# A delta-rule attention kernel with routed experts: the router's logits stay where the product leaves them, one row write a chunk, and a newly sought order

## The chip, the core and the metric

The kernel runs on one core of a Trainium2 chip. The metric is device time of one execution in microseconds (us); lower is better.

## What is computed

First, for 4 batches and 8 heads, a delta-rule attention over 768 steps with head size 48: with the key k normalised, y_t = q_t S, then S = S + beta_t k_t (v_t - S k_t). The heads' outputs, joined, are x with 384 columns per token. Then a mixture of 8 experts. logits = x w_gate; a local gate (one more column of weights) says whether a token takes the arg max of its own logits or the expert of the token before it in its sequence, so the choice is a running "last fresh choice" along the sequence. The output row is p[e] * relu(x w1[e]) w2[e], with p the softmax of the token's logits at its expert.

## The kernel before, in words

**Attention.** The 768 steps are 12 chunks of 64 steps; two chunks form a pair (0 to 5). A chunk's tokens lie on the 128 partitions as 64c+32a+t (c: which batch of two, a: which half of the chunk, t: step in the half), with a free index j for the other batch bit. For each pair a unit-triangular system is solved step by step (lines 293 to 306, "S" operations, 31 steps of two operations, 15 for pair 0). A table `MODE` says on which engine: all pairs on POOL (GpSimd), pair 3 on DVE (VectorE). Behind the solve stand transposes (lines 311, 314) and small products that make `XT` (lines 339 to 367). The chunks are then run in sequence by `online` (line 373): products with the state (fk, fq), the difference R (line 383), the product with `XT` (p1, line 391), the copy Us (line 397), the new state (p3, lines 400 to 404), the output (p2, lines 406 to 411) into the tile `y`. All these matmuls are issued through line 213.

**A chunk's way to the router.** `y` is written to the row table `xs` in DRAM by four transfers (line 415), transposed by one transfer into `xt` (line 417), multiplied with the router's weights (`lf`, line 422), and two DVE operations (line 438) put the logits into the tile `lt`, of which there is one. Eight transfers (line 442) then carry `lt` into `lg`, whose layout has one 32-step piece of one batch on 32 partitions. The last chunk writes `lg` without transfers: its product (`lf2`, line 429) is cut into 48 small matmuls, each aimed at its own 32 partitions. All these transfers are issued by SP (SyncE) in one queue.

**Routing** (lines 617 to 748) runs in two halves: the first when 8 chunks (16 columns of `lg`) are there, the second at the end. A half takes arg max and gates (629 to 637), finds the last fresh choice along the sequence by a transpose, a scan, a product with a block matrix (645) and a second scan (648), gives each token its expert and rank, and makes index lists for the gathers. Line 719 multiplies the exponentials with the chosen expert's mask; the planner may put it on DVE or POOL. 256 tokens of the first expert run behind the first half, the rest behind the second; from expert 2 on (`rest`) the order is fixed by hand.

**What sets the order.** A list scheduler (`Sched.order`) gives each operation an engine and a place when the program is built; on the chip each engine runs its own list in order and waits where an input is late. It uses estimated durations: 60 ns of SP for a transfer's issue, 2000 ns plus bytes over 330 bytes/ns to landing, and a model of TensorE's instruction fetch and clock. Between operations that could start it picks by the longest path behind them plus the offsets of the table `RANK` (by kind of operation and chunk), with `PACE` as a wished distance between successive p1. Buffers are given out in the same pass.

Of the kernel before, what the change touches and what calls it, by code (L numbers as in the profile page):

```python
# [36 lines left out]
class Op:  # L37
    def __init__(s,fn,bufs,e,c):
        s.lock=0; s.pc=None; s.fn=fn; s.bufs=bufs; s.e=e; s.c=c if isinstance(c,dict) else {x:c for x in e}
        s.pre=set(); s.succ=[]; s.end=None; s.iss=60.; s.takes=fn.__code__.co_argcount>len(fn.__defaults__ or ())  # L40

class Sched:


    HOP=70; DMA=2000; BW=330.; LOOK=120; WIN=3413.; UP=4.3; DN=3.6; FQ=128; FL=96; FT=2800.
# [28 lines left out]
    def span(s,o,t):  # L74

        if not o.pc: return o.c['P']
        c,w,n,q=o.pc; k=int(t//s.WIN)
        while len(s.hot)<=k:
            m=len(s.hot)-1; s.hot.append(s.act.get(m,0)>=(s.DN if s.hot[m] else s.UP))
        d=(w if s.hot[k] else c)/q; a,b=s.got,s.got+q; s.got=b; e=t  # L80
        while a<b:
            z=a%s.FQ; y=min(b,a-z+(s.FL if z<s.FL else s.FQ))
            if z==0: s.got_at=e
            if z==s.FL: e=max(e,s.got_at+s.FT)
            e+=d*(y-a); a=y
        return e-t
# [5 lines left out]
    def order(s):  # L92
        s.hot=[False]; s.act={}; s.got=0; s.got_at=0.
        s.rank(); E={x:0. for x in 'VAGPSL'}; dma=0.; out=[]; left={}; s.when=[]
# [54 lines left out]
class Attn:  # L149
# [3 lines left out]
    NKV=3; NW=14; NAMP=6; NG2=6; NXT=3; NLX=2; NUS=2; PACE=7526.1; MODE=((16,'G'),(32,'G'),(32,'G'),(32,'D'),(32,'G'),(32,'G'))  # L153
    RANK={'':{-1: -330.6},
# [50 lines left out]
    def build(s,extra=(),pre={},post=None):  # L205
# [167 lines left out]
        def online(n):  # L373
# [49 lines left out]
            def lf2():  # L423
                for a in range(2):
                    for b in range(4):
                        j,c=divmod(b,2); o=slice(64*c+32*a,64*c+32*a+32)
                        for z in range(2):
                            for kk in range(3):
                                nc.tensor.matmul(p.t[32*b:32*b+32,18*a:18*a+18-9*z],xt.t[:,6*j+3*z+kk,o],wv(kk,z),start=(z==0 and kk==0),stop=(z==1 and kk==2),skip_group_check=True,tile_position=(0,32*b))
            last=n==N-1  # L430
            add(lf2 if last else lf,r=[xt,"wc"],w=[p],e='P',c=900); S.ops[-1].pc=(900,850,.2,48) if last else (800,700,.6,12); C["lf"]=S.ops[-1]
            pv=lambda:p.t[:,0:36].rearrange("p (b w e) -> p b w e",b=2,w=2); lk=[("lg",2*n),("lg",2*n+1)]
            if last:
                def fg(): v=pv(); o=s.lg[:,2*n:2*n+2,:]; nc.vector.tensor_scalar_mul(o,v[:,:,0,:],2.0**-16); nc.vector.scalar_tensor_tensor(o,v[:,:,1,:],2.0**-16,o,op0=ALU.mult,op1=ALU.add)
                add(fg,r=[p],w=lk,c=370); s.lastfg=S.ops[-1]
            else:
                lt=s.lt()
# [22 lines left out]
class Moe:  # L460
# [14 lines left out]
    def consts(s):  # L475
# [119 lines left out]
    def graph(s,S,A):  # L595
# [21 lines left out]
        for z,(lo,hi) in enumerate(((0,SP),(SP,NS))):  # L617
# [27 lines left out]
            add(lambda pt=pt,dg=dg,n=n:nc.tensor.matmul(pt.t[:,0:n],s.blk,dg[:,0:n],start=True,stop=True),r=["sc"+Z,CK],w=[pt],e='P',c=450)  # L645
# [1 line left out]
            def fc(pt=pt,n=n,lo=lo,hi=hi,sl=sl,scT=scT,z=z):
                V.tensor_tensor_scan(s.cs[:,lo+1:hi+1],s.one.to_broadcast([128,n]),pt.t[:,0:n],0.0 if z==0 else s.cs[:,lo:lo+1],ALU.mult,ALU.max)
                V.tensor_tensor(s.ei[:,sl],scT[:,0:n],s.cs[:,lo:hi],op=ALU.max)
# [1 line left out]
            add(fc,r=[pt,"st"+Z,CK]+(["cs0"] if z else []),w=["cs"+Z,"ei"+Z],c=600)
# [3 lines left out]
            if z==0:  # L655
# [361 lines left out]
```

## Time and profile before

| | |
|---|---|
| median of 3 runs | 549.89 us (541.59, 550.07, 549.89) |
| profiled execution | 541.3 us, span 539.6 us, mean granted TensorE clock 0.819 |
| PE (matmul) / DVE / ACT / POOL busy | 409.8 / 337.6 / 188.5 / 234.6 us |
| transfers `lg<-lt`, `xs<-y`, `xt<-y` | 88, 48, 12 issues |

The span has two parts. Up to about 306 us attention and routing run, with all engines partly idle. From there the experts' matmuls follow each other closely. Times in rows count from the span's start. An engine name with q (SPq) is the engine's sequencer, which issues transfers and waits. In brackets behind a row of a timeline stands how long the engine idled before it and what ended that.

### The profile page before, as it was taken

To read this page: it belongs to the slowest core of one execution; us is meant where nothing else is said; L and a number is where in the kernel's file an instruction comes from. 1 tells how busy PE (TensorE), PEld (TensorE's weight loads), DVE (VectorE), ACT (ScalarE), POOL (GpSimd) and SP (SyncE) were. 2 spreads that over 40 slices of the span, in tenths; PEclk is the share of its full clock that TensorE was granted. 3 is DMA by queue.
4 is the path that set the end of the run, shared out by engine and by line. 5 is a ranking of instruction groups with operands and counts; after the bars stand their busy time and mean duration, and the time that the engine had idled before them with its cause. 6 is when DMAs were issued, how large, how long until landed. Compare 5 with 4: busy or idle time off the path is not lost. (4 is left out here: it accounts for less than half of the span.)

```text
span 539.6 us, 19450 instructions
## 1 busy us (share of the span) xinstructions
PE 409.8 (76%) x8459; PEld 304.6 (56%) x8459; DVE 337.6 (63%) x727; ACT 188.5 (35%) x332; POOL 234.6 (43%) x411
## 2 busy tenths in 40 slices
PE   4635785763766676677788598789999998999992
PEld 4534674752665676576675574354655555555661
DVE  3897145788985733693458545617666886778540
ACT  5323246424347343424540124305234251525210
POOL 5488889820797896141001543123141505040301
PEclk9665588796597665565599699899999999999997
DMA  8920054474275375255532295235655666385300
GB/s 329 388 91 5 5 121 106 122 183 113 82 232 126 94 194 114 55 125 114 168 91 60 76 201 178 81 122 156 176 169 151 197 162 205 101 251 138 73 16 26
DMA packets 68280, 72.78 MB, mean 135 GB/s; under 512 B 46771, under 2 KB 58095, under 8 KB 68192
## 3 DMA queue, kind: packets, MB, share of 16 engines
q1 hardware_dynamic: 64640, 61.45, 41.6%
q0 software_dynamic: 3552, 10.06, 5.9%
q8 instruction: 67, 1.10, 0.8%
q14 instruction: 21, 0.17, 0.1%
HBM read 52.63 MB, written 10.05 MB: 116 GB/s over the span
## 5 line engine op out<-in xcount | busy, mean ns | idle before, releaser
L298 POOL TENSOR_TENSOR fg<-L,X 128x31 f32<-128x31 f32 (+15 forms) x124 | 67.8, 547 | 35.3 <-DVE X L283 25.8
L299 POOL TENSOR_TENSOR X<-X,fg 128x31 f32<-128x31 f32 (+15 forms) x124 | 71.5, 577 | 9.7
L566 PEld LDWEIGHTS <-W 128*128 128x128 f16 (+2 forms) x408 | 41.5, 102 | 25.2 <-issue 0.5
L561 DVE TENSOR_SCALAR gf<-pr 128x384 f32<-128x384 f32 (+6 forms) x72 | 39.9, 556 | 24.5 <-ACT W L560 11.9
L559 PE MATMUL pr<-kv,amp 128*128 128x448 f16 (+4 forms) x192 | 53.9, 357 | 0.7 <-DVE tx L842 0.4
L213 PE MATMUL pr<-W 64*64 64x128 f32 x768 | 33.4, 329 | 22.8 <-DMA W<-in_kq_dram 11.5
L213 PE MATMUL pr<-S,W 64*64 64x48 f32 x1408 | 37.9, 273 | 13.0 <-issue 5.4
L213 PEld LDWEIGHTS pr<-S,W 64*64 64x64 f32 x1408 | 34.4, 188 | 16.2 <-issue 6.7
L213 PEld LDWEIGHTS pr<-W 64*64 64x64 f32 x768 | 29.1, 168 | 25.2 <-issue 8.0
L559 PE MATMUL pr<-kv,W 128*128 128x384 f16 (+2 forms) x144 | 38.0, 345 | 5.1 <-DVE tx L842 2.4
L559 PEld LDWEIGHTS <-W 128*128 128x128 f16 x288 | 29.4, 103 | 17.3 <-issue 4.0
L560 ACT ACTIVATE W<-pr 128x224 f16<-128x224 f32 (+3 forms) x32 | 15.5, 484 | 66.8 <-PE pr L559 64.8
L549 POOL DMA_INDIRECT out_dram<-y,so x9 | 10.7, 1187 | 53.4 <-DVE y L576 53.4
L547 POOL DMA_INDIRECT G<-xs,gi x25 | 26.2, 1050 | 13.0 <-issue 6.7
L213 PE MATMUL pr<-R,xtp 64*64 64x48 f32 x704 | 30.0, 251 | 1.8 <-issue 1.7
L213 PEld LDWEIGHTS pr<-R,xtp 64*64 64x64 f32 x704 | 28.8, 169 | 2.2 <-issue 2.2
L559 PEld LDWEIGHTS <-amp 128*128 128x128 f16 x192 | 18.8, 98 | 18.9 <-issue 1.9
L544 DVE SCALAR_TENSOR_TENSOR W<-W,W 128x768 f16<-128x768 f32 (+1 forms) x19 | 21.0, 1104 | 11.5 <-ACT W L542 11.4
L213 PE MATMUL pr<-Us,amp 64*64 64x48 f32 x768 | 19.2, 259 | 10.0 <-ACT Us L397 9.2
L549 POOL DMA_INDIRECT out_dram<-S,so x8 | 11.2, 1403 | 31.2 <-DVE S L576 29.3
L560 ACT ACTIVATE xtp<-pr 128x384 f16<-128x384 f32 (+2 forms) x16 | 8.4, 526 | 45.7 <-PE pr L559 41.1
L213 PEld LDWEIGHTS pr<-Us,amp 64*64 64x64 f32 x768 | 17.6, 174 | 11.8 <-ACT Us L397 10.8
(359 smaller groups left out, 987.1 us busy)
## 6 DMA issues: line engine op xcount, KB each, us to landing
W<-in_kq_dram SPq DMA_DIRECT2D x24, 512.0 KB, 6.5
W<-in_moe_w_dram SPq DMA_DIRECT2D x22, 512.0 KB, 4.9
W<-in_moe_w_dram SPq DMA_DIRECT2D x28, 384.0 KB, 3.3
kv<-in_kv_dram SPq DMA_DIRECT2D x12, 768.0 KB, 5.1
xs<-y SPq DMA_DIRECT2D x48, 96.0 KB, 2.8
amp<-in_moe_w_dram SPq DMA_DIRECT2D x4, 384.0 KB, 3.6
lg<-lt SPq DMA_DIRECT2D x88, 1.1 KB, 2.5
amp<-in_moe_w_dram SPq DMA_DIRECT2D x2, 512.0 KB
```

Source lines behind the costliest of these rows:

```text
L213: mm=lambda o,l,r,st,sp,tp:MM(o,l,r,start=st,stop=sp,skip_group_check=True,tile_position=tp)
L298: eng.tensor_tensor(tv,l[:,j,j+1:].unsqueeze(2).to_broadcast([128,n,k]),x[:,j,0:k].unsqueeze(1).to_broadcast([128,n,k]),op=ALU.mult)
L299: eng.tensor_tensor(x[:,j+1:,0:k],x[:,j+1:,0:k],tv,op=ALU.subtract)
L544: def wlo(s,st,w,k): s.nc.vector.scalar_tensor_tensor(s.wv(w,k)[:,1],s.wst(st,k),256.0,s.wv(w,k)[:,0],op0=ALU.mult,op1=ALU.subtract)
L547: return s.nc.gpsimd.indirect_dma_start(out=x[0:m],out_offset=None,in_=s.xs[0:nt,:],in_offset=bass.IndirectOffsetOnAxis(ap=ix[0:m],axis=0) ...
L549: I=s.nc.gpsimd.indirect_dma_start(out=s.out[:,:],out_offset=bass.IndirectOffsetOnAxis(ap=ix[0:m],axis=0),in_=y[0:m],in_offset=None,bounds ...
L559: for k in range(3): s.nc.tensor.matmul(ps,s.wv(W[k],k)[:,a,0,128*f:128*f+128],xT[:,3*b+k,:],start=(x==0 and k==0),stop=(x==2 and k==2))
L560: def uphi(s,h,ps): s.nc.scalar.activation(h,ps,AF.Relu,scale=2.0**-6)
L561: def upt(s,t,ps): s.nc.vector.tensor_scalar(t,ps,0.0,2.0**-6,op0=ALU.max,op1=ALU.mult)
L566: s.nc.tensor.matmul(po[0:m],h(a,f)[:,c:c+m],s.wv(W[k],k)[:,b,f%2,:],start=(x==0 and f==0),stop=(x==2 and f==7))
```

## The change

Every chunk's logits are now written by the two DVE operations straight into `lg`, in the layout that the product leaves (partition 64c+32a+t, column 2n+j). `lt`, its 88 transfers and the cut product `lf2` are gone; the last chunk uses the same 12 matmuls as the others. The row table follows the same layout, so a chunk's rows go out with one transfer in place of four. The routing is adapted: the mask `dm` is doubled to tell the two half-pieces apart, the block matrix covers 64 columns, the product of line 645 has twice the columns, and the function `fc` has three DVE operations more (a copy, a masked maximum, and the scan done once for each j). Constants (`first`, `s8`, `vals`, `am`) follow the layout. The planner counts 430 ns for a transfer's issue (1490 for the transpose, before 1700), includes all matmuls in its model of the instruction fetch and lets a fetch wait for transfers; `PACE` and `RANK` have new values, so the place of any operation up to the hand-ordered part can differ. `MODE` is as before.

```diff
 class Op:
-        s.lock=0; s.pc=None; s.fn=fn; ...
+        s.lock=0; s.pc=None; s.q=24; s.fn=fn; ...
-        ... s.iss=60.; ...
+        ... s.iss=430.; ...
 class Sched:
-    ... FT=2800.
+    ... FT=2400.; FD=450.
     def span(s,o,t):
-        if not o.pc: return o.c['P']
-        c,w,n,q=o.pc; k=int(t//s.WIN)
+        c,w,n,q=o.pc or (o.c['P'],o.c['P'],0.,o.q); k=int(t//s.WIN)
...
-            if z==0: s.got_at=e
+            if z==0: s.got_at=max(e+s.FD,s.dma)
...
-    ... PACE=7526.1; MODE=((16,'G'),(32,'G'),(32,'G'),(32,'D'),(32,'G'),(32,'G'))
+    ... PACE=11107.4; MODE=((16,'G'),(32,'G'),(32,'G'),(32,'D'),(32,'G'),(32,'G'))
-    RANK={'':{-1: -330.6},
...
+    RANK={'':{-1: 91.5, 0: -760.0},
...
-            for c in range(2):
-                for a in range(2):
-                    add(lambda c=c,a=a:nc.sync.dma_start(s.xs[2*n+a].rearrange(...)[c],y.t[64*c+32*a:64*c+32*a+32]...),...,c=98304)
+            add(lambda:nc.sync.dma_start(s.xs[2*n:2*n+2].rearrange("j p e -> p j e"),y.t.rearrange("p j z c -> p j (z c)")),...,c=393216)
-            def lf2(): ...
-            last=n==N-1
-            add(lf2 if last else lf,r=[xt,"wc"],w=[p],e='P',c=900); ...
+            add(lf,r=[xt,"wc"],w=[p],e='P',c=900); ...
-            if last:
-                def fg(): ...
-            else:
-                lt=s.lt()
-                def fg(): v=pv(); nc.vector.tensor_scalar_mul(lt.t,...); nc.vector.scalar_tensor_tensor(lt.t,...)
-                add(fg,r=[p],w=[lt],c=370); s.lastfg=S.ops[-1]
-                for j in range(2):
-                    for c in range(2):
-                        for a in range(2): add(lambda j=j,c=c,a=a:nc.sync.dma_start(s.lg[64*j+32*c:64*j+32*c+32,2*n+a,:],lt.t[...]),r=[lt],p=[lk[a]],claim=[lt],e='S',c=8192)
+            def fg(): v=pv(); o=s.lg[:,2*n:2*n+2,:]; nc.vector.tensor_scalar_mul(o,...); nc.vector.scalar_tensor_tensor(o,...)
+            add(fg,r=[p],w=lk,c=370); s.lastfg=S.ops[-1]
...
             def fs(...):
-                V.tensor_scalar(dg[:,0:n],s.dm[:,0:n],sc[:,31:32],None,op0=ALU.mult)
+                V.tensor_scalar(dg[:,:,0:n],s.dm[:,:,0:n],sc[:,31:32],None,op0=ALU.mult)
...
-                V.tensor_tensor_scan(s.cs[:,lo+1:hi+1],s.one.to_broadcast([128,n]),pt.t[:,0:n],...,ALU.mult,ALU.max)
-                V.tensor_tensor(s.ei[:,sl],scT[:,0:n],s.cs[:,lo:hi],op=ALU.max)
+                h0,h1=lo//2,hi//2; w=lambda x:x.rearrange("p (n j) -> p j n",j=2); k0=w(kt[:,0:n]); k1=w(pt.t[:,n:2*n])
+                V.tensor_copy(kt[:,0:n],pt.t[:,0:n]); V.scalar_tensor_tensor(scT[:,0:n],kt[:,0:n],s.am[:,0:1],scT[:,0:n],op0=ALU.mult,op1=ALU.max)
+                for j in range(2): V.tensor_tensor_scan(s.cs[:,j,h0+1:h1+1],k0[:,j],k1[:,j],...,ALU.max,ALU.max)
+                V.tensor_tensor(w(s.ei[:,sl]),w(scT[:,0:n]),s.cs[:,:,h0:h1],op=ALU.max)
```

## Rows read from the trace of the kernel before

**Rows 1.** Stretch, length; busy us of PE, PEld, DVE, ACT, POOL; clock, DMA share, GB/s
```profile
61.00:110.00 49.00, 35.48 (x1470) 32.80 (x1470) 25.69 (x55) 25.42 (x51) 42.80 (x80) 0.79 0.45 109
...
205.00:241.00 36.00, 25.10 (x802) 23.23 (x802) 21.60 (x55) 11.68 (x20) 13.71 (x24) 0.55 0.45 91
...
306.00:531.00 225.00, 209.49 (x1393) 123.82 (x1391) 142.04 (x248) 67.56 (x107) 63.31 (x54) 0.98 0.52 145
```

**Rows 2.** Waits of POOL: total us, times, longest us
```profile
POOL fg L298 <- DVE X L283: 25.8, 2, 23.8
...
POOL fg L302 <- DVE wc L229: 11.2, 1, 11.2
```

**Rows 3.** Timeline of POOL around the solve of pair 5: start, us
```profile
175.67 1.04 POOL L298 TENSOR_TENSOR fg<-L,X 128x31 f32<-128x31 f32 x1 [1.95 <-DVE X L283]
...
227.31 0.63 POOL L719 TENSOR_TENSOR kf<-kf,oh 128x128 f32<-128x128 f32 x1 [15.43 <-DVE oh L652]
...
235.52 0.25 POOL L299 TENSOR_TENSOR X<-X,fg 128x31 f32<-128x31 f32 x1
```

**Rows 4.** Timeline of SP's queue, chunks 6, 7, 8 and 10, 11
```profile
203.36 6.29 SPq L442 DMA_DIRECT2D lg<-lt  x8
209.76 1.52 SPq L417 DMA_TRANSPOSE xt<-y  x1
...
215.78 5.29 SPq L442 DMA_DIRECT2D lg<-lt  x8
...
244.31 6.69 SPq L442 DMA_DIRECT2D lg<-lt  x8
252.91 0.40 SPq L584 DMA_DIRECT2D amp<-in_moe_w_dram  x1
...
276.27 5.85 SPq L442 DMA_DIRECT2D lg<-lt  x8
282.23 1.45 SPq L417 DMA_TRANSPOSE xt<-y  x1
```

**Rows 5.** Timeline of DVE: outputs of chunks 7 and 11, first routing
```profile
203.32 0.96 DVE L411 SCALAR_TENSOR_TENSOR y<-pr,y 128x768 f16<-128x768 f32 x1
...
215.57 0.18 DVE L438 SCALAR_TENSOR_TENSOR lt<-pr,lt 128x18 f32<-128x18 f32 x1
...
222.29 0.29 DVE L629 TENSOR_REDUCE mxl<-lg 128x16 f32<-128x128 f32 x1 [1.36 <-DMA lg<-lt]
...
225.50 0.19 DVE L648 TENSOR_TENSOR_SCAN cs<-one,pr 128x16 f32<-128x16 f32 x1
...
280.39 0.95 DVE L411 SCALAR_TENSOR_TENSOR y<-pr,y 128x768 f16<-128x768 f32 x1
```

**Rows 6.** The transfers of lines 442 and 415: duration of an issue, ns min/median/max
```profile
L442 SPq DMA_DIRECT2D lg<-lt x88: 507/589/1710, 84.7 to 281.5; - x88
...
L415 SPq DMA_DIRECT2D xs<-y x48: 303/432/1788, 76.0 to 285.6; - x48
```

**Rows 7.** Waits of PE between 205 and 259 us: total us, times, longest
```profile
PE pr L213 <- issue: 6.0, 5, 2.5
PE pr L555 <- ACT W L760: 2.6, 1, 2.6
...
PE pr L645 <- DVE sc L646: 2.1, 1, 2.1
PE pr L555 <- DVE lt L438: 1.5, 1, 1.5
```

**Rows 8.** Timeline of PE: p1 of chunks 9, 10, 11, the last logit product
```profile
231.62 1.51 PE L213 MATMUL pr<-R,xtp 64*64 64x48 f32 x45
...
259.01 3.65 PE L213 MATMUL pr<-R,xtp 64*64 64x48 f32 x64
...
273.38 2.05 PE L213 MATMUL pr<-R,xtp 64*64 64x48 f32 x64
...
285.93 0.79 PE L429 MATMUL pr<-wc,xt 128*32 128x18 f16 x48 [1.43 <-DMA xt<-y]
```

More of the change, by code (lines that the diff above doesn't have):

```diff
@@ L38, in __init__ @@
     def __init__(s,fn,bufs,e,c):
-        s.lock=0; s.pc=None; s.fn=fn; s.bufs=bufs; s.e=e; s.c=c if isinstance(c,dict) else {x:c for x in e}
-        s.pre=set(); s.succ=[]; s.end=None; s.iss=60.; s.takes=fn.__code__.co_argcount>len(fn.__defaults__ or ())
+        s.lock=0; s.pc=None; s.q=24; s.fn=fn; s.bufs=bufs; s.e=e; s.c=c if isinstance(c,dict) else {x:c for x in e}
+        s.pre=set(); s.succ=[]; s.end=None; s.iss=430.; s.takes=fn.__code__.co_argcount>len(fn.__defaults__ or ())
 class Sched:
-    HOP=70; DMA=2000; BW=330.; LOOK=120; WIN=3413.; UP=4.3; DN=3.6; FQ=128; FL=96; FT=2800.
+    HOP=70; DMA=2000; BW=330.; LOOK=120; WIN=3413.; UP=4.3; DN=3.6; FQ=128; FL=96; FT=2400.; FD=450.
     def __init__(s): s.ops=[]; s.links=[]; s.gaps=[]; s.tag=('',0); s.bias={}; s.wr={}; s.rd={}; s.pw={}
@@ L92, in order @@
     def order(s):
-        s.hot=[False]; s.act={}; s.got=0; s.got_at=0.
-        s.rank(); E={x:0. for x in 'VAGPSL'}; dma=0.; out=[]; left={}; s.when=[]
+        s.hot=[False]; s.act={}; s.got=1; s.got_at=0.; s.dma=0.
+        s.rank(); E={x:0. for x in 'VAGPSL'}; out=[]; left={}; s.when=[]
         todo=[o for o in s.ops]
@@ L133, in order @@
             if x in 'SI':
-                dma=max(dma,t)+o.c[x]/s.BW; o.end=dma+(s.DMA if x=='S' else 2500)
+                s.dma=max(s.dma,t)+o.c[x]/s.BW; o.end=s.dma+(s.DMA if x=='S' else 2500)
             else: o.end=t+busy+(190 if x=='P' else s.HOP)
@@ L422, in lf, with fg @@
                         for kk in range(3): nc.tensor.matmul(p.t[:,18*j:18*j+18-9*z],xt.t[:,6*j+3*z+kk,:],wv(kk,z),start=(z==0 and kk==0),stop=(z==1 and kk==2),skip_group_check=True)
[L423 to L429, printed above, removed]
-            last=n==N-1
-            add(lf2 if last else lf,r=[xt,"wc"],w=[p],e='P',c=900); S.ops[-1].pc=(900,850,.2,48) if last else (800,700,.6,12); C["lf"]=S.ops[-1]
-            pv=lambda:p.t[:,0:36].rearrange("p (b w e) -> p b w e",b=2,w=2); lk=[("lg",2*n),("lg",2*n+1)]
-            if last:
-                def fg(): v=pv(); o=s.lg[:,2*n:2*n+2,:]; nc.vector.tensor_scalar_mul(o,v[:,:,0,:],2.0**-16); nc.vector.scalar_tensor_tensor(o,v[:,:,1,:],2.0**-16,o,op0=ALU.mult,op1=ALU.add)
-                add(fg,r=[p],w=lk,c=370); s.lastfg=S.ops[-1]
-            else:
-                lt=s.lt()
-                def fg(): v=pv(); nc.vector.tensor_scalar_mul(lt.t,v[:,:,0,:],2.0**-16); nc.vector.scalar_tensor_tensor(lt.t,v[:,:,1,:],2.0**-16,lt.t,op0=ALU.mult,op1=ALU.add)
-                add(fg,r=[p],w=[lt],c=370); s.lastfg=S.ops[-1]
-                for j in range(2):
-                    for c in range(2):
-                        for a in range(2): add(lambda j=j,c=c,a=a:nc.sync.dma_start(s.lg[64*j+32*c:64*j+32*c+32,2*n+a,:],lt.t[64*c+32*a:64*c+32*a+32,j,:]),r=[lt],p=[lk[a]],claim=[lt],e='S',c=8192)
+            add(lf,r=[xt,"wc"],w=[p],e='P',c=900); S.ops[-1].pc=(800,700,.6,12); C["lf"]=S.ops[-1]
+            pv=lambda:p.t[:,0:36].rearrange("p (b w e) -> p b w e",b=2,w=2); lk=[("lg",2*n),("lg",2*n+1)]
+            def fg(): v=pv(); o=s.lg[:,2*n:2*n+2,:]; nc.vector.tensor_scalar_mul(o,v[:,:,0,:],2.0**-16); nc.vector.scalar_tensor_tensor(o,v[:,:,1,:],2.0**-16,o,op0=ALU.mult,op1=ALU.add)
+            add(fg,r=[p],w=lk,c=370); s.lastfg=S.ops[-1]
         for m in range(-1,NM):
@@ L483, in consts @@
         s.lotc=K([128,E],F32,"lotc"); s.c512=K([128,E],F32,"c512")
-        s.one=K([128,1],F32,"one"); s.c256=K([128,1],F32,"c256"); s.dm=K([128,32],F32,"dm"); s.seg=K([128,E,SP],F32,"seg"); s.vals=K([128,NS,5],F16,"vals")
-        s.kp_=[K([128,32],F32,"kp%d"%z) for z in range(2)]; s.cs=K([128,NS+1],F32,"cs")
+        s.one=K([128,1],F32,"one"); s.c256=K([128,1],F32,"c256"); s.dm=K([128,2,32],F16,"dm"); s.am=K([128,1],F32,"am"); s.seg=K([128,E,SP],F32,"seg"); s.vals=K([128,NS,5],F16,"vals")
+        s.kp_=[K([128,32],F32,"kp%d"%z) for z in range(2)]; s.cs=K([128,2,NS//2+1],F32,"cs")
         def f0(): make_identity(nc,s.ident)
@@ L490, in f1 @@
             nc.gpsimd.memset(s.blk,0.0); nc.gpsimd.memset(s.dm,0.0); nc.gpsimd.memset(s.one,1.0); nc.gpsimd.memset(s.c256,256.0)
-            for b in range(4): nc.gpsimd.memset(s.blk[32*b:32*b+32,32*b:32*b+32],1.0)
+            nc.gpsimd.memset(s.am,0.0)
+            for b in range(4): nc.gpsimd.memset(s.blk[32*b:32*b+32,64*(b//2):64*(b//2)+64],1.0); nc.gpsimd.memset(s.am[32*b:32*b+32],float(b%2))
         def f2():
@@ L497, in f2 @@
             for b in range(4):
-                nc.gpsimd.memset(s.first[32*b:32*b+1,0:1],1.0)
+                if b%2==0: nc.gpsimd.memset(s.first[32*b:32*b+1,0:2],1.0)
                 q=slice(32*b,32*b+32)
-                nc.gpsimd.affine_select(out=s.dm[q],in_=s.one[q].to_broadcast([32,32]),pattern=[[1,32]],compare_op=ALU.is_equal,fill=0.0,base=0,channel_multiplier=-1)
+                nc.gpsimd.affine_select(out=s.dm[q,b%2],in_=s.one[q].to_broadcast([32,32]),pattern=[[1,32]],compare_op=ALU.is_equal,fill=0.0,base=0,channel_multiplier=-1)
             nc.gpsimd.memset(s.seg,1.0); nc.gpsimd.memset(s.seg[:,:,0:1],0.0)
-            nc.gpsimd.memset(s.lotc,0.0); nc.gpsimd.memset(s.lotc[:,0:1],float(s.LOT)); nc.gpsimd.memset(s.cs[:,0:1],0.0)
+            nc.gpsimd.memset(s.lotc,0.0); nc.gpsimd.memset(s.lotc[:,0:1],float(s.LOT)); nc.gpsimd.memset(s.cs,0.0)
             for t in s.kp_: nc.gpsimd.memset(t,0.0)
-            for b in range(4): nc.gpsimd.memset(s.vals[32*b:32*b+32,:,2:3],float((s.SEQ-32)*b))
+            vj=s.vals.rearrange("p (n j) v -> p j n v",j=2)
+            for b in range(4): nc.gpsimd.memset(vj[64*(b%2):64*(b%2)+64,b//2,:,2:3],float((2*s.SEQ-32)*(b//2)+(s.SEQ-64)*(b%2)))
         def f3():
@@ L609, in graph @@
         tq=[K([128,2,24],F32,"tq%d"%z) for z in range(3)]; rhs_=K([128,NS,2,5],F16,"rhs")
-        scs=[[K([128,32],F32,"sc%d"%i) for i in range(4)]]*2
+        scs=[[K([128,2,32] if i==2 else [128,32],F32,"sc%d"%i) for i in range(4)]]*2
         OB=s.OB=A.obp(); OB2=A.ob2()
@@ L641, in fs, with fc @@
                 V.transpose(kt,kp); V.tensor_tensor_scan(sc,s.one.to_broadcast([128,32]),kt,0.0,ALU.mult,ALU.max)
[L642 removed]
+                V.tensor_scalar(dg[:,:,0:n],s.dm[:,:,0:n],sc[:,31:32],None,op0=ALU.mult)
             add(fs,r=["kp"+Z,CK]+(["cs0"] if z else []),w=["sc"+Z],c=600)
             pt=A.pt()
[L645 removed]
+            add(lambda pt=pt,dg=dg,n=n:nc.tensor.matmul(pt.t[:,0:2*n].rearrange("p (a i) -> p a i",a=2),s.blk,dg[:,:,0:n],start=True,stop=True),r=["sc"+Z,CK],w=[pt],e='P',c=450); S.ops[-1].q=2
             add(lambda scT=scT,sc=sc:V.transpose(scT,sc),r=["sc"+Z],w=["st"+Z])
[L647 to L649 removed]
+            def fc(pt=pt,n=n,lo=lo,hi=hi,sl=sl,scT=scT,z=z,kt=kt):
+                h0,h1=lo//2,hi//2; w=lambda x:x.rearrange("p (n j) -> p j n",j=2); k0=w(kt[:,0:n]); k1=w(pt.t[:,n:2*n])
+                V.tensor_copy(kt[:,0:n],pt.t[:,0:n]); V.scalar_tensor_tensor(scT[:,0:n],kt[:,0:n],s.am[:,0:1],scT[:,0:n],op0=ALU.mult,op1=ALU.max)
+                for j in range(2): V.tensor_tensor_scan(s.cs[:,j,h0+1:h1+1],k0[:,j],k1[:,j],0.0 if z==0 else s.cs[:,j,h0:h0+1],ALU.max,ALU.max)
+                V.tensor_tensor(w(s.ei[:,sl]),w(scT[:,0:n]),s.cs[:,:,h0:h1],op=ALU.max)
                 V.tensor_single_scalar(s.ei[:,sl],s.ei[:,sl],E-1,op=ALU.bitwise_and)
[L651 removed]
+            add(fc,r=[pt,"st"+Z,CK]+(["cs0"] if z else []),w=["cs"+Z,"ei"+Z],c=1100)
             add(lambda oh=oh,sl=sl,n=n:V.tensor_tensor(oh,s.ib[:,0:E].unsqueeze(2).to_broadcast([128,E,n]),s.ei[:,sl].unsqueeze(1).to_broadcast([128,E,n]),op=ALU.is_equal),r=["ei"+Z],w=["oh"+Z])
@@ L733, in fq @@
                     for i in range(r0,r1): nc.tensor.matmul(q.t[:,0:2*nv].rearrange("p (a c) -> p a c",a=2),ob(i),rhs_[:,i,:,c0:c1],start=(i==r0),stop=(i==r1-1))
-                add(fq,r=obk+[("rhs",part,x) for x in ((0,) if z==0 else (0,SP))],w=[q],claim=[OB,OB2],e='P',c=50*(r1-r0))
+                add(fq,r=obk+[("rhs",part,x) for x in ((0,) if z==0 else (0,SP))],w=[q],claim=[OB,OB2],e='P',c=50*(r1-r0)); S.ops[-1].q=r1-r0
                 def fin(q=q,part=part,a0=a0,z=z,nv=nv,hi=hi):
```

18 lines of the change are left out of this document (9 added, 9 removed), and 34 rows, old and new, of the table RANK.

## The prediction

> **What bounds the kernel now.** I first read busy time by stretch. From 306 us to the last matmuls PE is busy 209.5 of 225 us at clock 0.98 [rows 1]: the experts run against PE, nothing of the change touches their work, and whatever is won or lost earlier shifts this block as a whole. Before it no engine is full: between 205 and 241 us PE is busy 25.1 of 36 us and POOL 13.7 [rows 1]. So the place to look is the end of the attention stage, and the question for each engine is what its next instruction in line waits for.
>
> Second, the waits of POOL. Its list holds the solves; two long waits stand among them: 23.8 us before pair 4 [rows 2] and, inside the solve of pair 5, 15.4 us [rows 3]. The second is not the solve's own: line 719, a step of the first routing half, stands in POOL's list ahead of the last steps of pair 5 and waits for the mask of line 652. The solve then ends at 235.8 us and not 15 us sooner.
>
> Third, why that mask was late, followed back over SP and DVE. The output of chunk 7 was ready at 203.32 + 0.96 = 204.28 us [rows 5]; its transpose was issued at 209.76, because SP was putting out the eight logit transfers of chunk 6 from 203.36 to 209.65 [rows 4]. That is 5.5 us. The logits of chunk 7 stood in lt at 215.57 + 0.18 = 215.75 us, and the first routing operation began at 222.29, when the transfers had landed [rows 5]: 6.5 us. Together 12.0 us of the 15.4.
>
> Fourth, the waits of PE from 205 to 259 us [rows 7]: 6.2 us are in sight of the same cause. The product of line 645 stood in PE's list and waited 2.1 us for the routing; a transpose waited 1.5 us for lt, which was not free until the burst of 244.31 to 251.00 had landed; another waited 2.6 us for an ACT copy that stood behind a weight whose load SP issued at 252.91, after that burst [rows 4, 7]. A further 6.0 us is "issue", which I leave alone.
>
> **The change part by part.**
>
> *Transfers removed.* 88 issues of 0.589 us, 51.8 us of SP; 48 row writes of 0.432 us become 12. No row shows the issue of one write of this shape; between the shortest 0.30 and the longest 1.79 us seen for a write [rows 6] I take the median, so 36 x 0.432 = 15.6 us go. These 67 us are not the gain: SP isn't the bound, only the three places above are. The same bytes go to xs. Larger pieces could land later; gathers of the first half wait for the index list anyway, which follows the whole routing chain.
>
> *The routing chain of the first half.* 5.5 us (transpose) and 6.5 us (landing) go. Added are three DVE operations on tiles of 16 columns or fewer: at the 0.19 us of the scan [rows 5] that is 0.6 us. The doubled mask and the doubled columns of line 645 are within that. Net 11.4 us. POOL's wait falls from 15.4 to 4.0 us, and the solve of pair 5 would end at 224.4 us.
>
> *How much of it reaches the path.* The order is new, so the trace can't show it; bounds. Below: the routing's first operation stands behind a weight split on DVE, and idled only 1.36 us for the transfers [rows 5]. If the new list keeps those two in that order, 1.4 us is won. Above: p1 of chunk 10 follows p1 of chunk 9 by 27.4 us, while chunk 11 follows 10 by 14.4 us [rows 8], a pair's second member needing no new solve. So at most 13.0 us can go before the chain from state to state binds instead; that is what is late next. Between them: PE's own waits of 6.2 us go where they stand; and with pair 5 solved earlier, the small products behind it can fill pauses of PE, which has 10.9 us of them in 205 to 241. I take 10.0, nearer to the upper end because 12.0 us of delay is read directly from two queues and the planner places the routing by when its inputs come.
>
> Here the clock has to be weighed. In 205 to 241 us the granted clock was 0.55, nearly all at 1.2 GHz; in 61 to 110 us 0.79, with PE busy 72% against 70% [rows 1]. Busy share does not order the two, so I count no gain from closing pauses. The Trainium skill, TensorE: Matmul & The Clock Gate, section "Part 1: The HAM clock gate", says that half clock is the resting state and that the array's own activity releases it. By that rule the sum would be lower than mine; no row here proves it.
>
> *The last chunk.* Its output was ready at 280.39 + 0.95 = 281.34 us, its transpose issued at 282.23 behind the burst of chunk 10 [rows 4, 5]: 0.9 us. Its product has 12 matmuls in place of 48; at 0.79 us for 48 [rows 8] that saves 0.6. The second routing half pays 0.6 us for its three operations, on the path. Net 0.9 us gained.
>
> *Constants.* A handful of POOL memsets more, hidden by the 11.2 us POOL waits before its first solve [rows 2]; without that cover they would cost well under a microsecond.
>
> *The new order elsewhere.* The 23.8 us pause before pair 4 [rows 2] could shrink or another could open. Ends: 24 us less; as much more. I take zero, since no row speaks for a side.
>
> **Sum.** 10.0 + 0.9 = 10.9 us off the profiled execution's own 541.3 us (span 539.6): 530.4. That execution agrees with the lowest run shown, 541.59; the median, 549.89, is 1.6% above it, and I forecast in terms of the profiled one. Two per cent, about 11 us, is what a measurement of this kernel can tell from no change, so the forecast stands at that edge.
>
> **Rivals.**
>
> *The chain or the list holds (539 us).* The new list leaves the routing behind DVE's weight work, or PE's in-order list spends the freed time elsewhere: 1.4 + 0.9 us won, 541.3 - 2.3 = 539. For it: the 1.36 us; and PE waits 6.0 us for issue, which the change doesn't touch. Against: line 719's 15.4 us is a wait on exactly the data that now comes sooner.
>
> *The clock rises too (523 us).* If the closed pauses bring 205 to 241 us from 0.55 to 0.79, its 25.1 us of PE work takes 25.1 x 0.55 / 0.79 = 17.5, 7.6 us less: 530.4 - 7.6 = 523; the same time would come if the pause before pair 4 shrank by a third. For it: both levels appear in this stage at like load. Against: like load, unlike clock, so load alone doesn't decide. The skill's rule of above is on the side of this rival.
>
> *Slower (558 us): line 719 stands earlier in POOL's list.* In POOL's order it holds up every solve step behind it. The solve of pair 5 took 235.77 - 175.67 - 15.43 = 44.7 us without its wait [rows 3]. With the routing 12.0 us sooner less its own 0.6, the mask comes at about 215.9 us. Were line 719 ahead of the first step, the solve would end at 215.9 + 44.7 = 260.6, 24.8 us later than now: 541.3 + 24.8 - 0.9 = 565. It decides from where the solve ends 11 us later than now, that is with more than 31 of the 44.7 us behind it: 552. I name 558, the middle. For it: the list before made this error by 15 us. Against: a greedy planner puts it there only if it believes the routing done by then, and the largest things it misjudged, SP's issues, are gone.
>
> That the transfers aren't removed is no case; the code has none left.
>
> **How the numbers follow.** Forecast (525 to 536) 0.42; rival "holds" (536 to 546) 0.26; clock or a better order (513 to 525) 0.18; slower 0.14. Faster by over 2% than 541.3 means below 530.5: all of the third case and 0.27 of the forecast's 0.42 (a little over half, as the direct reading of the two queues, 12.0 us, lies above the 10.0 taken): 0.45. Slower by over 2%: most of the last case, 0.13. Within: 0.42. Single number 530.5; range 514 to 546, which leaves out most of the slower case and the edge of the third.
>
> **What would show it.** Right: no SP issue between a chunk's output and its transpose; the first routing operation within 2 us of the logits of chunk 7; POOL's wait at line 719 below 5 us; p1 of chunk 10 less than 20 us behind that of chunk 9; the PE-full block starting near 295 us with the same length. Wrong: a new wait of more than 5 us in POOL's solves or between p1 of 9 and 10; a granted clock in 61 to 110 us well below its 0.79, which would cost what is won later.

## The result, and the profile after

| kernel | median, us (lowest to highest) | ratio to before, 95% interval |
|---|---|---|
| before | 548.06 (541.59 to 550.07) | |
| after | 523.14 (522.56 to 525.05) | 0.9624 [0.9541, 0.9707] |

The change made the kernel 3.8% faster. The profiled executions are 541.3 us (span 539.6) and 522.56 us (span 520.8): 18.7 us less, against a forecast of 10.9. The experiments show that the time did not come from where the forecast put most of it.

Windows of the kernel after, with the columns of [rows 1]; its dense block begins earlier, so the third window is moved:

```profile
61.00:110.00 49.00, 34.42 (x1304) 32.44 (x1304) 30.28 (x70) 21.61 (x45) 42.73 (x81) 0.71 0.37 106
205.00:241.00 36.00, 26.66 (x1011) 24.97 (x1003) 25.60 (x81) 16.29 (x29) 19.47 (x33) 0.64 0.41 101
291.00:512.00 221.00, 206.78 (x1392) 122.76 (x1391) 142.56 (x249) 67.30 (x106) 61.33 (x53) 0.99 0.53 147
```

The first dense matmuls, timeline of PE before, then after:

```profile
306.12 3.15 PE L559 MATMUL pr<-amp,W 128*128 128x224 f16 x16
```
```profile
290.97 2.40 PE L542 MATMUL pr<-xtp,W 128*128 128x224 f16 x12
```

PE's last matmul ends at 529.3 us before and at 510.4 after. So 15.1 us were won ahead of the dense block, and the block itself takes 219.4 in place of 223.2 us, 3.8 less. (One profile used below, that of kept_719, is of an execution 1.6% above its kernel's fastest; only the order of events within it and their distances are used.)

SP's queue after, chunks 7, 8 and 11, to be read against [rows 4]:

```profile
201.19 1.59 SPq L414 DMA_TRANSPOSE xt<-y  x1
202.83 0.72 SPq L412 DMA_DIRECT2D xs<-y  x1
203.60 0.47 SPq L567 DMA_DIRECT2D W<-in_moe_w_dram  x1
...
222.14 1.44 SPq L414 DMA_TRANSPOSE xt<-y  x1
...
264.96 1.44 SPq L414 DMA_TRANSPOSE xt<-y  x1
```

DVE after, to be read against [rows 5]: the output of chunk 7, its logits, the first routing operation, the product that was line 719.

```profile
200.22 0.94 DVE L410 SCALAR_TENSOR_TENSOR y<-pr,y 128x768 f16<-128x768 f32 x1
...
212.34 0.18 DVE L422 SCALAR_TENSOR_TENSOR lg<-pr,lg 128x18 f32<-128x18 f32 x1
212.56 0.29 DVE L612 TENSOR_REDUCE mxl<-lg 128x16 f32<-128x128 f32 x1
...
219.81 0.38 DVE L704 TENSOR_TENSOR kf<-kf,oh 128x128 f32<-128x128 f32 x1
```

The transpose is issued 0.03 us after the output (200.22 + 0.94 = 201.16) and the routing begins 0.04 us after the logits. POOL's waits after (total, times, longest), against [rows 2, 3]:

```profile
POOL S L704 <- DVE oh L637: 37.5, 1, 37.5
POOL fg L297 <- DVE X L282: 30.6, 2, 29.1
```

The new list has the first half's line 704 (719 before) on DVE, so nothing interrupts the solve of pair 5. The pause before pair 4 became longer, 29.1 against 23.8 us. The 37.5 us stand in the second half, after the solves. p1 of chunks 9 to 11 and the last logit product after, against [rows 8]:

```profile
223.13 1.05 PE L212 MATMUL pr<-R,xtp 64*64 64x48 f32 x30
...
246.71 2.05 PE L212 MATMUL pr<-R,xtp 64*64 64x48 f32 x34
...
257.56 0.65 PE L212 MATMUL pr<-R,xtp 64*64 64x48 f32 x16
268.92 0.45 PE L419 MATMUL pr<-wc,xt 128*128 128x18 f16 x12
```

From chunk 9 to 10 it is still 23.6 us (27.4 before).

### The profile page after: what moved, and what is told of

The parts are those of the page before. It is cut to its first block, busy times and chain, and to the rows that moved or that the text cites. A ratio compares the mean times of both kernels' runs of the same rounds, so it can differ in the third digit from the quotient of the medians.

```text
span 520.8 us, 19200 instructions
## 1 busy us (share of the span) xinstructions
PE 400.9 (77%) x8423; PEld 299.3 (57%) x8423; DVE 341.5 (66%) x738; ACT 186.5 (36%) x330; POOL 229.8 (44%) x411
## 5 line engine op out<-in xcount | busy, mean ns | idle before, releaser
L298 POOL TENSOR_TENSOR X<-X,fg 128x31 f32<-128x31 f32 (+15 forms) x124 | 74.3, 599 | 9.7
L549 PEld LDWEIGHTS <-W 128*128 128x128 f16 (+2 forms) x492 | 49.5, 101 | 35.7 <-issue 5.1
L543 ACT ACTIVATE W<-pr 128x384 f16<-128x384 f32 (+6 forms) x56 | 26.7, 481 | 113.8 <-PE pr L542 102.2
L544 DVE TENSOR_SCALAR gf<-pr 128x384 f32<-128x384 f32 (+6 forms) x72 | 40.0, 556 | 23.8 <-ACT W L543 10.7
L542 PE MATMUL pr<-kv,W 128*128 128x384 f16 (+3 forms) x192 | 50.4, 343 | 3.9 <-DVE tx L827 2.2
L212 PEld LDWEIGHTS pr<-W 64*64 64x64 f32 x768 | 28.3, 167 | 28.3 <-issue 10.4
L542 PEld LDWEIGHTS <-W 128*128 128x128 f16 x336 | 33.5, 101 | 18.2 <-issue 1.0
L530 POOL DMA_INDIRECT G<-xs,gi x25 | 26.2, 1046 | 14.9 <-DVE pvs L832 7.0
L542 PE MATMUL pr<-kv,amp 128*128 128x448 f16 (+2 forms) x120 | 31.0, 351 | 0.6 <-issue 0.4
L549 PE MATMUL Sps<-W,W 128*128 128x384 f16 (+2 forms) x126 | 24.5, 326 | 4.2 <-DVE kf L559 4.2
L542 PE MATMUL pr<-kv,xtp 128*128 128x496 f16 (+2 forms) x72 | 25.5, 355 | 0.0
L259 DVE TENSOR_TENSOR amp<-pr,mask 128x512 f32<-128x512 f32 x24 | 16.4, 684 | 12.8 <-ACT gt L256 5.7
L410 DVE SCALAR_TENSOR_TENSOR y<-pr,y 128x768 f16<-128x768 f32 x12 | 11.4, 952 | 20.4 <-ACT y L409 20.4
```

What stands on the lines that cost most here:

```text
L212: mm=lambda o,l,r,st,sp,tp:MM(o,l,r,start=st,stop=sp,skip_group_check=True,tile_position=tp)
L259: add(lambda n4=n4,gv=gv:nc.vector.tensor_tensor(n4(am.t),gv()[:,:,:,64:128],s.mask.unsqueeze(1).unsqueeze(1).to_broadcast([128,2,4,64]),o ...
L298: eng.tensor_tensor(x[:,j+1:,0:k],x[:,j+1:,0:k],tv,op=ALU.subtract)
L410: add(lambda:nc.vector.scalar_tensor_tensor(y.t[:,:,1,:],py.t[:,:,0:384],256.0,y.t[:,:,0,:],op0=ALU.mult,op1=ALU.subtract),r=[py,(y,0)],w= ...
L530: return s.nc.gpsimd.indirect_dma_start(out=x[0:m],out_offset=None,in_=s.xs[0:nt,:],in_offset=bass.IndirectOffsetOnAxis(ap=ix[0:m],axis=0) ...
L542: for k in range(3): s.nc.tensor.matmul(ps,s.wv(W[k],k)[:,a,0,128*f:128*f+128],xT[:,3*b+k,:],start=(x==0 and k==0),stop=(x==2 and k==2))
```

## Experiments

Each ratio is against runs of the kernel before on the same chip (medians 545.6 to 547.6 us).

### First four: data flow, order, and line 719 apart

**kept_flow**: the new data flow (logits straight to `lg`, one row write, the new routing), every engine's list in the order before. Lines of before, in short:

```diff
-  for b,a: add(lambda j=j,c=c,a=a:nc.sync.dma_start(s.lg[...],lt.t[...]),...)
+  for b,a: add(lambda:None,...)          # keeps its place in the planner, emits nothing
-  def fg(): ... lt.t ...
+  def fg(): ... s.lg[:,2*n:2*n+2,:] ...
```

> The list of every engine is that of the kernel before, place by place; only the 88 logit transfers are gone, four row writes are one, the last logit product has 12 matmuls, and the routing is that of the changed kernel. Queue theory (the time went into what stood behind SP's transfers): the waits of PE in 205 to 259 us that hang on them (1.5, 2.6, part of 2.1) and 0.9 us at the last transpose go, the routing begins 1.4 to 6 us sooner: 530 to 536 us against 541.3 of the profiled execution before. Order theory (the gain is in the newly sought list): 538 to 542, since every engine still waits in the old places.

**flow_only**: the kernel after with the planner's old model, `RANK` and `PACE`, which plan the new flow afresh.

```diff
-    PACE=11107.4; RANK={... after ...}; iss=430.
+    PACE=7526.1; RANK={... before ...}; iss=60.
```

> The changed kernel's data flow (no logit transfers, one row write a chunk), ordered by the planner with all its old numbers (issue 60 ns, old model of the fetch, old RANK and PACE). Queue theory: 522 to 532 us, nearly the whole gain. Order theory: 535 to 548, since offsets sought for another list of operations fit this one badly.

**order_only**: the kernel before with the new model, `RANK` and `PACE`.

```diff
-    PACE=7526.1; RANK={... before ...}; iss=60.
+    PACE=11107.4; RANK={... after ...}; iss=430.
```

> The data flow of the kernel before (88 logit transfers, four row writes a chunk), ordered by the planner with all its new numbers (issue 430 ns, new model of the fetch, new RANK and PACE). Queue theory: 536 us or more, since the transfers still stand in SP's queue. Order theory: 523 to 532.

**kept_719**: the kernel before, its order kept, the first half's product of line 719 on DVE in place of POOL.

```diff
-  add(lambda e,...:e.tensor_tensor(ex(),ex(),ohT(),op=ALU.mult),...)
+  add(lambda e,...,z=z:(e if z else V).tensor_tensor(ex(),ex(),ohT(),op=ALU.mult),...)
```

> The kernel before with one operation moved: the first half's product of line 719 runs on DVE at the place it has in the order, not on POOL, so that POOL's solve of pair 5 has no wait of 15.4 us in it. If that wait sets the end of the attention stage, as my prediction took for most of its 10 us: 529 to 535 us. If PE's own list sets it (PE waited 1.0 us for the solve's results at 241 us): 538 to 542.

| kernel | median, us | ratio, 95% interval |
|---|---|---|
| kept_flow | 530.51 | 0.9725 [0.9640, 0.9811] |
| flow_only | 529.94 | 0.9733 [0.9654, 0.9812] |
| order_only | 553.65 | 1.0162 [1.0046, 1.0278] |
| kept_719 | 544.79 | 0.9957 [0.9907, 1.0008] |

The data flow alone gives 2.7%, planned afresh or not. The new planner numbers alone cost 1.6%. And POOL's wait at line 719 is worth at most 0.9%. Two traces say the same of it. In kept_719 the solve of pair 5 has no wait inside: it begins at 179.62 and ends at 223.07 us, 43.5 us for 60.1 in [rows 3]. And p1 of chunk 10 still comes 26.7 us after that of chunk 9. POOL, then PE of kept_719:

```profile
222.23 0.84 POOL L299 TENSOR_TENSOR X<-X,fg 128x31 f32<-128x31 f32 x1
```
```profile
236.07 1.51 PE L213 MATMUL pr<-R,xtp 64*64 64x48 f32 x45
...
262.78 3.44 PE L213 MATMUL pr<-R,xtp 64*64 64x48 f32 x60
```

In kept_flow the wait is nearly as long as before, and the gain is there all the same. POOL of kept_flow, then its p1 of chunks 8 to 11:

```profile
222.15 0.62 POOL L723 TENSOR_TENSOR kf<-kf,oh 128x128 f32<-128x128 f32 x1 [13.57 <-DVE oh L656]
```
```profile
212.78 0.99 PE L213 MATMUL pr<-R,xtp 64*64 64x48 f32 x14
...
226.21 0.64 PE L213 MATMUL pr<-R,xtp 64*64 64x48 f32 x8
...
251.87 0.56 PE L213 MATMUL pr<-R,xtp 64*64 64x48 f32 x6
...
263.62 0.59 PE L213 MATMUL pr<-R,xtp 64*64 64x48 f32 x14
```

Against before (chunk 8 at 215.19, and [rows 8]) kept_flow is ahead by 2.4, 5.4, 7.1 and 9.8 us at chunks 8, 9, 10, 11. From 9 to 10, where the forecast put nearly all, it wins 1.7.

### Next four: is it SP's queue, the landing, or the planner?

Two theories for the 2.7%. Q: the transfers fill SP's queue, and what stands behind them is late. L: the work that waits for their landing, and for the single `lt`, is late.

**kept_burst**: kept_flow, with the 88 transfers at their old places, now into a tile that nobody reads.

```diff
-  add(lambda:None,...)
+  add(lambda j=j,c=c,a=a:nc.sync.dma_start(s.wc[64*j+32*c:64*j+32*c+32,a,:],s.lg[64*c+32*a:64*c+32*a+32,2*n+j,:]),...)
```

> The kernel with the new data flow in the old order (530.5 us, 0.9725 of before), and the 88 transfers issued again at their old places in SP's list, from the logits tile into a tile that nobody reads. Every engine's list is otherwise that of the kernel in the old order. Theory Q (the transfers cost by filling SP's queue: transposes and weight loads stand behind them): the gain is mostly lost, 538 to 544 us, ratio to before 0.985 to 1.0; transposes again issued 4 to 6 us after their output. Theory L (they cost by what waits for their landing: the routing and the single tile lt): 529 to 533 us, ratio 0.97 to 0.975, although SP is as full as before. Both in part: about 535.

**kept_lt2**: the kernel before, the logits of odd chunks staged in a second tile.

```diff
-  lt=s.lt();   ... fg writes lt.t
+  lt=s.lt(); lv=(lambda lt=lt:lt.t) if n%2==0 else (lambda:s.wc[:,0:2,:])   ... fg writes lv()
```

> The kernel before with one thing changed: the logits of odd chunks go to a second tile in place of the single lt, so that a chunk's logits no longer wait for the landing of the previous chunk's eight transfers. All transfers stay, order unchanged. If the single tile is the main cost (PE stands behind a product whose PSUM place is not drained): 532 to 538 us, ratio 0.975 to 0.985. Theory Q and the landing before the routing: 543 to 546 us, ratio 0.995 to 1.0.

**after_burst**: the kernel after, eight unread transfers behind each chunk's logits.

```diff
+  def burst(): ... for j,c,a: nc.sync.dma_start(s.wc[64*j+32*c:64*j+32*c+32,a,:],s.lg[64*c+32*a:64*c+32*a+32,2*n+j,:])
-  def fg(): ...
+  def fg(): ...; burst()
```

> The changed kernel with eight unread transfers behind each chunk's logits (all but the last), at that place in SP's list; every other engine's list is unchanged. Theory Q: 5 to 10 us slower than the changed kernel, 528 to 534 us, ratio to before 0.967 to 0.98. Theory L: 523 to 525 us, ratio 0.958 to 0.965.

**model_flow**: the kernel after, only `RANK` and `PACE` old.

```diff
-    PACE=11107.4; RANK={... after ...}
+    PACE=7526.1; RANK={... before ...}
```

> The changed kernel with the old RANK and PACE but the new numbers of the planner's model (430 ns an issue, all matmuls in the fetch model). With the old numbers throughout it took 529.9 us (0.9733 of before). If the better model makes the remaining 1.1 per cent: 522 to 526 us, ratio 0.957 to 0.965, and fetch idle of PE before the dense block near 24 us instead of 38. If the searched offsets RANK make it: 528 to 534 us, 0.967 to 0.98; old offsets under a model they were not sought for may even be worse, to 540.

| kernel | median, us | ratio, 95% interval |
|---|---|---|
| kept_burst | 545.04 | 0.9893 [0.9808, 0.9978] |
| kept_lt2 | 545.90 | 0.9964 [0.9917, 1.0011] |
| after_burst | 542.13 | 0.9891 [0.9815, 0.9968] |
| model_flow | 552.09 | 1.0116 [1.0074, 1.0158] |

Transfers that nobody waits for take back 14.5 us of the old order by the medians (12.7 without kept_burst's longest run, 551.54 us) and 19.0 us of the new one. After_burst loses about twice what Q expected (5 to 10 us). In its trace ACT waits 26.2 us for weights into one tile (`amp`) where the kernel after waits 7.1. Theory L, which expected 523 to 525 us there and 529 to 533 in kept_burst, falls: what kept_burst keeps of the change (no landing to wait for, no `lt`, fewer row writes, 12 matmuls in the last product) is worth 0.2 to 1.9%, a second `lt` alone at most 0.8%. Model_flow is worse than either theory of it said.

### Last four: issuing or pieces, early or late

**kept_one**, **kept_tiny**, **kept_late** differ from kept_burst in the unread transfers alone:

```diff
 kept_one:  one transfer a chunk
+  nc.sync.dma_start(s.wc[:,0:3:2,:],s.lg[:,2*n:2*n+2,:])
 kept_tiny: eight transfers of one partition
+  nc.sync.dma_start(s.wc[64*j+32*c:64*j+32*c+1,a,:],s.lg[64*c+32*a:64*c+32*a+1,2*n+j,:])
 kept_late: the eight of kept_burst, chunks 6 to 10 only
+  ... if n>=6 else (lambda:None)
```

> The kernel with the new data flow in the old order (530.5 us without any logit transfer, 545.0 us with eight unread transfers a chunk), and in place of the eight one unread transfer a chunk of the same bytes in the same 256 pieces of 36 bytes. Nothing else in any engine's list differs. If the eight transfers cost by the time that SP spends on issuing them: 529 to 534 us, ratio to before 0.97 to 0.978. If they cost by their pieces on the DMA engines, delaying other transfers and PE's instruction fetch: 540 to 546 us, ratio 0.985 to 1.0.

> The same with eight unread transfers a chunk again, each of one partition's 36 bytes in place of 32 partitions': SP issues as many as before, the DMA engines have 1/32 of the bytes. Cost by SP's issuing: 540 to 546 us, ratio 0.985 to 1.0, if an issue takes as long as before (0.5 to 0.7 us); with shorter issues (0.3 to 0.4 us) 535 to 540. Cost by the pieces on the DMA engines: 529 to 533 us.

> The kernel with eight unread transfers a chunk, but only for chunks 6 to 10: 40 transfers, from about 185 us on. The prediction put the whole cost there (a transpose 5.5 us late behind the burst of chunk 6, weight loads behind that of chunk 8): if so, 541 to 545 us, ratio 0.985 to 0.998. If every burst costs about alike, through the small delays of 61 to 185 us too: 530.5 + 14.5 x 40/88 = 537 us, ratio 0.98 to 0.985. If only the early ones cost: 530 to 532.

**rank_flow**: the kernel after with the planner's old model, `RANK` and `PACE` new.

```diff
-    iss=430. ... FT=2400.; FD=450. (and the fetch model)
+    iss=60. ... FT=2800.
```

> The changed kernel with the new RANK and PACE but the old numbers of the planner's model (60 ns an issue and the old fetch model). Old model with old RANK took 529.9, new with new 523.1, new with old 552.1 us. If RANK and PACE are sought for one model and only good with it: 535 to 555 us, ratio 0.98 to 1.02. If they carry the 1.1 per cent by themselves: 522 to 526 us, ratio 0.957 to 0.965.

| kernel | median, us | ratio, 95% interval |
|---|---|---|
| kept_one | 527.95 | 0.9657 [0.9564, 0.9750] |
| kept_tiny | 544.61 | 0.9991 [0.9943, 1.0039] |
| kept_late | 535.10 | 0.9813 [0.9739, 0.9888] |
| rank_flow | 546.79 | 1.0020 [0.9969, 1.0071] |

All bytes in one issue a chunk cost nothing; eight issues with 1/32 of the bytes cost everything, 16.7 us. So the cost goes with the number of issues, and SP's time for issuing is the reading that the queue's rows support; a cost of each transfer outside SP was not tried apart. The transfer's line in kept_burst, kept_one and kept_tiny (duration of an issue, ns min/median/max, first and last start):

```profile
L442 SPq DMA_DIRECT2D wc<-lg x88: 507/589/1607, 86.2 to 279.7; - x88
```
```profile
L442 SPq DMA_DIRECT2D wc<-lg x11: 605/620/1268, 84.4 to 264.2; - x11
```
```profile
L442 SPq DMA_DIRECT2D wc<-lg x88: 688/689/1646, 85.8 to 285.2; - x88
```

kept_late lies between. It has 40 of the 88 transfers and loses 7.2 us to kept_one, where kept_tiny loses 16.7 on the same chip; against kept_flow it is 4.6 of kept_burst's 14.5 us. So the cost goes about with the number of bursts, and much of it arises with those of chunks 0 to 5, behind which no transpose was more than 0.13 us late in kept_tiny. A delay behind an early burst is seen at chunk 3. SP's queue there in before, kept_flow and kept_tiny:

```profile
121.22 5.91 SPq L442 DMA_DIRECT2D lg<-lt  x8
127.23 0.53 SPq L369 DMA_DIRECT2D kv<-in_kv_dram  x1
```
```profile
120.72 1.64 SPq L369 DMA_DIRECT2D kv<-in_kv_dram  x1
```
```profile
122.67 6.27 SPq L442 DMA_DIRECT2D wc<-lg  x8
129.05 0.41 SPq L369 DMA_DIRECT2D kv<-in_kv_dram  x1
```

DVE waits for that load in line 371, and POOL's solve of pair 4 waits for DVE. Both lines in before, kept_flow and kept_tiny, DVE first:

```profile
132.43 0.96 DVE L371 TENSOR_TENSOR kv<-kv,nT 128x768 f32<-128x768 f32 x1 [1.33 <-DMA kv<-in_kv_dram]
```
```profile
129.51 0.95 DVE L371 TENSOR_TENSOR kv<-kv,nT 128x768 f32<-128x768 f32 x1
```
```profile
134.44 0.96 DVE L371 TENSOR_TENSOR kv<-kv,nT 128x768 f32<-128x768 f32 x1 [2.80 <-DMA kv<-in_kv_dram]
```
```profile
136.16 0.51 POOL L298 TENSOR_TENSOR fg<-L,X 128x31 f32<-128x31 f32 x1 [23.84 <-DVE X L283]
```
```profile
133.23 0.51 POOL L298 TENSOR_TENSOR fg<-L,X 128x31 f32<-128x31 f32 x1 [20.81 <-DVE X L283]
```
```profile
138.18 0.51 POOL L298 TENSOR_TENSOR fg<-L,X 128x31 f32<-128x31 f32 x1 [25.58 <-DVE X L283]
```

kept_late, without a burst there, starts pair 4 at 133.43 us. That this delay costs time is not shown, and kept_one speaks against it: there the pause is 23.68 us, nearly that of before, and the kernel is as fast as kept_flow. Nor is pair 4 waited for soon: in before its solve ends near 173 us, and p1 of its first chunk, chunk 8, comes at 215.19. POOL of kept_one:

```profile
135.23 0.51 POOL L298 TENSOR_TENSOR fg<-L,X 128x31 f32<-128x31 f32 x1 [23.68 <-DVE X L283]
```

The second place is ACT, which splits expert weights between its copies for the attention, in one list. Its waits for weights from 61 to 300 us, in kept_one, then kept_tiny:

```profile
ACT W L544 <- DMA W<-in_moe_w_dram: 5.2, 2, 4.0
...
ACT W L544 <- DMA amp<-in_moe_w_dram: 0.5, 1, 0.5
```
```profile
ACT W L544 <- DMA W<-in_moe_w_dram: 8.5, 3, 4.6
ACT xtp L544 <- DMA W<-in_moe_w_dram: 7.1, 1, 7.1
...
ACT W L544 <- DMA amp<-in_moe_w_dram: 4.0, 2, 2.6
...
ACT amp L544 <- DMA amp<-in_moe_w_dram: 3.2, 1, 3.2
```

That is 5.7 against 22.8 us. These sums aren't the cost by themselves: kept_late has 24.7 us of such waits (at the same line) and loses less than half of what kept_tiny loses. What counts is what stands behind such a wait in ACT's list. Between p1 of chunks 10 and 11 it is the copy Us of chunk 10 (line 397), without which the chain from chunk to chunk cannot go on. SP, PE and ACT of kept_tiny, then PE and ACT of kept_one:

```profile
254.49 5.99 SPq L442 DMA_DIRECT2D wc<-lg  x8
260.71 0.37 SPq L586 DMA_DIRECT2D W<-in_moe_w_dram  x1
```
```profile
259.75 3.65 PE L213 MATMUL pr<-R,xtp 64*64 64x48 f32 x64
```
```profile
266.08 1.06 ACT L544 ACTIVATE xtp<-W 128x1024 f16<-128x1024 f32 x1 [7.10 <-DMA W<-in_moe_w_dram]
...
268.68 0.79 ACT L397 COPY Us<-pr 128x768 f32<-128x768 f32 x1
```
```profile
250.93 2.94 PE L213 MATMUL pr<-R,xtp 64*64 64x48 f32 x64
```
```profile
253.92 0.80 ACT L397 COPY Us<-pr 128x768 f32<-128x768 f32 x1 [1.13 <-PE pr L213]
```

In kept_tiny a weight's load is issued right behind the burst, ACT waits 7.10 us for it, and Us starts 5.3 us after p1 has ended (at 263.40); in kept_one it starts 0.05 us after. From p1 of chunk 10 to p1 of chunk 11 kept_tiny takes 17.3 us, kept_one 10.4. The same copy is late, behind a split that waited for a weight, in before at chunks 6, 8 and 10 (2.4, 1.1 and 2.6 us) and in kept_late at chunks 8 and 10 (1.6 and 4.2 us); in kept_flow it is never more than 0.1 us late. In after_burst Us of chunk 7 and the copy of the state behind chunk 10 (line 403 of the kernel after) are 6.2 us late each. Of the 10.4 us by which kept_flow reaches the dense block earlier than before, these copies are 6.1; where the rest went is not shown.

## Why the prediction was right, and where it was not

**The number.** 530.5 was forecast and the range held the time. By the prediction's own parts it stands otherwise: the data flow alone, in the order before, gives 530.5; the new planner numbers add the rest, 7.4 us, which the forecast counted at zero. That the forecast's single number is also 530.5 is luck, since its largest term did not hold.

**SP's queue: right in kind, too short in reach.** That the transpose and the weight loads stand behind bursts was read correctly [rows 4, 7], and undone bursts are what pays (kept_one against kept_tiny, 16.7 us). The prediction named three places, all after 203 us. It had the place at ACT too, as 2.6 us of a transpose on PE; but the copies Us stand in the same list of ACT, and held up the chain itself by 6.1 us at chunks 6, 8 and 10. It left out the kv loads, which share the queue: one stood 0.1 us behind a burst, with POOL's pause before pair 4 at its end. In kept_flow that pause is 20.8 us and not 23.8, but kept_one shows that this is not what pays.

**POOL's wait at line 719: the step that failed.** "I take 10.0 ... because 12.0 us of delay is read directly from two queues." The delay is real, but it wasn't on the path: with the wait gone the time is the same (kept_719), with the wait kept the gain comes (kept_flow). The prediction treated the end of the pair-5 solve as what p1 of chunk 10 waits for. The sign against it stood in [rows 8] and [rows 3]: the solve ended at 235.8, p1 came at 259.0. The 23 us between were other work, and it did not come sooner. Accordingly "p1 of chunk 10 less than 20 us behind" failed: 23.6. Nor was the upper bound one: it took the 14.4 us from p1 of chunk 10 to that of chunk 11 for the least distance, and it is 10.9 us after (10.4 in kept_one), since the 14.4 held a late copy Us of its own.

**The 10.0 came out at 10.4 for another sum.** The dense block of kept_flow starts 10.4 us earlier, measured at the last matmuls ahead of it (305.8 and 295.4). It builds up along the whole stage: p1 is 3.5 us ahead at chunk 4, 2.4 at chunk 8 and 9.8 at chunk 11. That the sum is near 10.0 is luck.

**Landing.** The 6.5 us went as said. Without them, but with SP as full as before, little is won: kept_burst, kept_tiny.

**Row writes.** The prediction priced the new write like an old one, 0.432 us. It takes 0.834 (median of 12), so 48 x 0.432 - 12 x 0.834 = 10.7 us of SP went, not 15.6. What the writes alone are worth was not tried.

**The last chunk.** The transpose is on time (0.9 us won). The product took 0.45 for 0.79 us, so it saved 0.3 and not 0.6.

**The dense block.** "The same length" failed by 3.8 us. PE's busy time in it fell from 209.49 to 206.78 us, and its idle time by 1.1. PE's longest wait there, before and after, is for the same kind of DVE operation:

```profile
PE Sps L566 <- DVE kf L576: 5.5, 4, 3.4
```
```profile
PE Sps L549 <- DVE kf L559: 4.9, 5, 1.4
```

Around it the granted clock was 0.83 before (346 to 356 us) and 1.00 after (331 to 341 us). From the last small matmul ahead of it the block takes 223.5 us before, 223.1 in kept_flow and 219.7 after. But this does not show that the new order did it: with the old order it takes 221.3 us in the profile of kept_late and 227.9 in that of kept_burst, with the new order 222.0 in after_burst. What makes the block shorter stays open, and that the shorter wait raised the clock was not tried.

**Clock.** The rival with 0.55 rising to 0.79 in 205 to 241 us gave the right time, 523, and was not what happened: 0.64 there, and 0.71 for 0.79 in 61 to 110 us, which the prediction had named as a sign of being wrong. The pause before pair 4 grew by 5.3 us as well; pair 4 starts at 140.8 us for 136.2, and the kernel is the faster one all the same.

**The slower rival.** The planner did not put line 719 earlier on POOL; it put it on DVE.

**Order.** Old model with old `RANK` 529.9, new with new 523.1, but new with old 552.1 and old with new 546.8. The offsets are good only with the model for which they were sought. Which of the moved operations carry the 1.3% (529.9 to 523.1) stays open. The intervals of the two ratios overlap, their runs do not (529.0 to 531.2 and 522.6 to 525.1 us). Of the 7.8 us between the two profiled executions 3.4 are the dense block's (223.1 us in flow_only, 219.7 after), whose length also differs between kernels of one order; the rest lies ahead of it, and no single wait accounts for it.

## What to carry to other kernels

A queue that issues transfers is a resource in order, like an engine: list for each burst every load behind it and who waits for that, not only the burst's own readers, and count issues before bytes. A long wait on an engine is a cost only if its end is what the next chain waits for: compare the end of the wait's work with the start of its reader, and look for the copies of that chain behind each wait in an engine's list. Keep an order and change the data flow, and the reverse, before giving a planner's new order the credit.

## What was not expected of the hardware

An issue on SP takes 0.62 us for 256 pieces of 36 bytes over 128 partitions, 0.59 for 32 partitions and 0.69 for one partition (medians): for these small transfers its time hardly depends on what it moves. It is not constant: a row write took 0.43 us for 96 KB before and 0.83 for 384 KB after. And less idle time of PE that nothing in the trace released did not go with less time: summed over such idles above 0.15 us, ahead of the dense block, it is 37.0 us before, 23.7 after, 23.4 in model_flow (552.1 us) and 16.7 in after_burst (542.1 us). In before 28 of these 29 idles come at the same place of every 256 instructions of PE, weight loads included: number 193 or 194, counted from 0. What PE waits for there the trace does not show.
